# One kernel, two stages: a new order for k's copies, token ranks and early weights, and the last two batches routed together

## The chip, the cores and the metric

The kernel runs on one core of a Trainium2 chip. The metric is device time in microseconds of one execution, 669.85 us as the median of three runs (667.71 to 671.05). The engines are named as the profile names them: PE (TensorE, matrix multiply; PEld is its weight load), DVE (VectorE), ACT (ScalarE), POOL (GpSimd), SP (SyncE, which here issues transfers). Each engine works through its own instructions in order.

## The reference

Two stages. The first is an attention over 8 batches, 8 heads, 576 positions of 64 numbers, done twice and added: once on means of four neighbouring positions (144 coarse positions, all against all, repeated four times), once between positions less than four apart. The second is a mixture of experts on the 4608 tokens of 512 numbers that come out: each token goes to one of 8 experts.

```python
def sm_attn(qq, kk, vv):                       # softmax(qq kk^T / 8) vv
    ...
out_up = np.repeat(sm_attn(q_d, k_d, v_d), 4, axis=2)      # *_d: means of four positions
mask = np.abs(pos[:, None] - pos[None, :]) < 4
out_local = softmax(where(mask, q k^T / 8, -1e9)) @ v
x = (out_up + out_local).transpose(0, 2, 1, 3).reshape(4608, 512)

logits = x @ w_gate + modality_bias[modality_id]
e_idx, gate_w = argmax(logits), max(softmax(logits))
for e in range(8):
    mask = e_idx == e
    h = np.maximum(x[mask] @ w1[e], 0.0)       # 512 -> 1024
    out[mask] = gate_w[mask, None] * (h @ w2[e])           # 1024 -> 512
```

## The kernel before

**The attention** runs in 32 steps of two heads each (four steps, n = 4b to 4b+3, are one batch b). What one step's heads need is spread over several steps, so that the engines work on different steps at once. The order is written by hand: `PHASE` gives each operation a time in units of a step, a call for step n gets the time n + phase, all calls are sorted by it, and each engine's instructions are issued in this order. The names that matter:

- `tpq`, `tpk`, `tpt`: PE transposes q and k into PSUM; `qT`, `kT`: ACT copies them into SBUF (`kT0` copies k in two halves of 64 partitions, L330); `kd`: DVE sums k by four.
- `sc`, `lm`, `le`, `exp`, `z`, `zr`, `nl`, `lt`, `Pw`, `avl`: the local part (scores on PE, maximum and difference on DVE, exponential on ACT, sums and their reciprocal on DVE, normalisation `nl` on POOL L426, a DVE transpose, a copy on ACT L442, the product with v on PE).
- `scd`, `dm`, `de`, `nd`, `pdt`, `PdT`, `avd`, `Od`: the same for the coarse part (`nd` on POOL L430, `pdt` PE transposes, `PdT` ACT copies). `vp`, `vc`: v's means. `X`: DVE adds both parts into the tile X of the batch (and `late`, the columns kept for the next batch).
- Routing of a batch, at phases of 7 and more, so some four steps behind its first head: `lg` (PE, the logits in two halves), `LT` (ACT copies), `lgt` (PE transposes), `L`, `ch1`, `ch2`, `gt` (small DVE instructions), `ex` (ACT), `pr` (PE, the rank of each token inside its expert), `pl` (DVE, its place), `st` (POOL: one indirect transfer a tile of 128 tokens, which scatters token number and gate into the table `tab`), `R` (DVE transposes X back to rows of tokens) and `W` (SP stores these rows into `xs`).

Some tiles of PSUM and SBUF turn in rings (tag T with three buffers, S with three, A with two), and an operation waits until the reader of the buffer's last content is done.

**The experts.** After four batches the tokens of the first half are counted (`first`, `early`), and an expert with many of them gets its first two units of 512 tokens early: `expert` and `entries` fetch its number and its list, `rows` gathers the tokens (POOL), `wload` and `wsplit` load its weights in eight chunks, c = 0 to 3 for the first layer, 4 to 7 for the second, and split each into a high and a low part (high on POOL for the first four, else on ACT L876; low on DVE L882). `split` turns the tokens' rows on PE and splits them. `raws` says which buffer (raw0 to raw2) a pair of chunks takes. Chunks with a turn from `HOLD` to `NHOLD` are issued behind the last batch's routing on ACT and DVE. Before, chunks 0 to 3 are handled in the attention and 4 to 7 after it; batch six is routed in the hand-written order, batch seven after it.

`compute` is a unit's first layer: eight blocks f of twelve matmuls (L1005) into PSUM, each followed by a relu on ACT (L1010) and its low part on DVE (L1011); `second` is the second layer (L1059), with a scaled copy (L1061) and an indirect transfer of the result. Then come three units of 1024 tokens (`Large`), two of 256 and one of 128, and a loop for what is left. Outside the hand-written part a planner with its own model of costs orders the instructions.

Of the kernel before, what the change touches and what calls it, by code (L numbers as in the profile page):

```python
# [7 lines left out]
F32 = mybir.dt.float32  # L8
# [4 lines left out]
ALU = mybir.AluOpType  # L13
# [34 lines left out]
NPW = 3  # L48
NR = 4
TB, SB = 3, 3  # L50
HOLD = 5
NHOLD = 8

QUADS = 3
# [4 lines left out]


PHASE = {
# [10 lines left out]
}  # L72


def whole(pieces):

    while True:
        try:
            next(pieces)
        except StopIteration as x:  # L80
            return x.value
# [116 lines left out]
class Attention:  # L198
# [120 lines left out]

    def kT_(s, n, i):  # L320
        g = n % 2
        p = s.t["tp", "t"][:, 1] if i else s.t["tp", "k", n]
        for a in range(2):
            r = slice(64 * a, 64 * a + 64)
            if i:
                t = s.kB[r].rearrange("m g a t -> m g (a t)")[:, :, KT * a + PAD : KT * a + PAD + 512 + 64]
                s.nc.scalar.copy(t[:, 0, 512:], p[r, :64])
                s.nc.scalar.copy(t[:, 1, :64], p[r, 64:])
            else:
                s.nc.scalar.copy(s.kB[r, g, a, PAD + 64 * g : PAD + 64 * g + 512], p[r])  # L330
# [167 lines left out]
class Router:  # L498
# [32 lines left out]
    def LT(s, b, hf):  # L531
        W = 64 * s.t["G", b]
        if ("LT", b) not in s.t:
            s.t["LT", b] = s.wk.tile([128, 640], F32, name="LT", bufs=1)
        s.nc.scalar.copy(s.t["LT", b][:, hf * W : (hf + 1) * W], s.t.pop(("lg", b, hf)))

    def lgt(s, b, i):
# [77 lines left out]
    def R(s, b, t):  # L615

        if t < s.t["G", b]:
            if t % 2 == 0:
                if b < B - 1:
                    x = s.rp.tile([128, 8, 4, 32], F32, name="R", bufs=NR)  # L620
                elif t == 4:
                    x = s.rp.tile([128, 4, 4, 32], F32, name="o", bufs=3)
                else:
                    x = s.block(f"G{2 + t // 2}", F32)[:, :1024].rearrange("p (i k c) -> p i k c", i=8, k=4)
                s.t["R", b, t // 2] = x
            R = s.t["R", b, t // 2][:, 4 * (t % 2) : 4 * (t % 2) + 4]
            s.nc.vector.transpose(R, s.t["X", b][:, :, 128 * t : 128 * t + 128].rearrange("p k (i j) -> p i k j", j=32))
# [178 lines left out]
class Moe:  # L806
    def __init__(s, tc, ctx, C, psum, xs, tab, w1, w2, out):
        s.tc, s.nc, s.C, s.ps = tc, tc.nc, C, psum
        s.xs, s.tab, s.w1, s.w2, s.out = xs, tab, w1, w2, out
        s.wr = ctx.enter_context(tc.tile_pool(name="mwr", bufs=1))  # L810
        s.wa = ctx.enter_context(tc.tile_pool(name="mwa", bufs=1))
        s.xa = ctx.enter_context(tc.tile_pool(name="mxa", bufs=1))
        s.turn = {}
        s.cw, s.after, s.before = 0, (), []
        s.raws = iter([0, 1, 2, 0] + [0, 2, 1] * 6)
        ring = ["G0", "G1", "G2", "G3", "H0", "H1", "H2", "H3", "V0", "V1", "V2", "V3", "H6", "H7"]
        s.wseq = iter(["H4", "H5", "H6", "H7", "V0", "V1", "V2", "V3"] + ring * 3)

# [168 lines left out]
    def compute(s, T, W, X, H=2, step=None, mid=None, J=None, last=0):  # L987
        nc = s.nc
        xh, xl = X
        hh, hl = s.hidden(H)  # L990
        N = 128 * H
        n = 4 // H
        early = H == 4 and s.turn["h"] == 0
        ps = {}
        for f, ks in [(f + j, k) for f in range(0, 8, 2) for k in ((0, 1), (2, 3)) for j in range(2)] if early else [
                (f, range(4)) for f in range(8)]:
            if step and f % 2 == 0 and 0 in ks:
                step()
            if f % n == 0 and 0 in ks:
                ps[f // n] = s.ps.tile([128, n, N], F32, name="l1", tag="S", bufs=SB)  # L1000
            p, fs = ps[f // n], slice(128 * f, 128 * f + 128)
            for k in ks:
                wh, wl = W[k]
                for i, (a, x) in enumerate(((wh, xh), (wh, xl), (wl, xh))):
                    nc.tensor.matmul(p[:, f % n, :], a[:, fs], x[:, k, :N], start=(k == 0 and i == 0),  # L1005
                                     stop=(k == 3 and i == 2))
            if f % n == n - 1 and 3 in ks:
                g = slice((f + 1 - n) % 4, f % 4 + 1)
                y, z = hh[f // 4][:, g, :N], hl[f // 4][:, g, :N]
                nc.scalar.activation(y, p, AF.Relu)  # L1010
                nc.vector.scalar_tensor_tensor(z, p, 0.0, y.bitcast(F32), op0=ALU.max, op1=ALU.subtract)  # L1011
        s.second(T, W[4:], hh, hl, H, step, mid, J, last)

    def compute_half(s, T, W, X, step, mid, J):
# [183 lines left out]
def build(tc, q, k, v, mid, w_gate, bias, w1, w2, out):  # L1198
    nc = tc.nc
    with ExitStack() as ctx:  # L1200
# [10 lines left out]
        with ExitStack() as actx:  # L1211
# [35 lines left out]
            def call(at, f, *args):  # L1247
                calls.append((at, len(calls), f, args))
# [8 lines left out]
            for nm, p in P.items():  # L1257
                f, i = (nm[:-1], int(nm[-1])) if nm[-1].isdigit() and nm not in ("ch1", "ch2") else (nm, 0)
                if f in batch:
                    for b in range(B - 1):  # L1260
                        late_ = {2: 0.05, 0: 0.9, 3: 0.14}.get(i, 0) if f == "st" and b == B - 2 else 0
                        call(4 * b + p + late_, getattr(ro, parts.get(f, f)), b, i)
                else:
                    for n in range(0, N, 2 if f in ("vp", "vc", "tpt") or nm in ("qT1", "kT1", "kd1") else 1):
                        call(n + p, values if f == "X" else getattr(at, parts.get(f, f)), n, i)
            for b in range(B):
                if b + 1 < B:
                    for j in range(2):
                        call(4 * b - 1 + used + 0.3 + 0.8 * j, at.load_v, b + 1, 4 * j)
            for h in range(3, N // 2):  # L1270
                call(2 * h - 5 + last + 0.25, at.load_qk, h // 2, h % 2)

# [57 lines left out]
            for u in range(KEARLY):  # L1330
                call(t + 1 + 0.1 * u, expert, u)
            for u in range(KEARLY):
                call(t + 1.5 + 0.1 * u, entries, u)
            for i in range(4):
                call(t + 4.75 + 0.3 * i, rows, 0, i)
            free = N - 1 + max(P["scd"], P["sc0"], P["sc1"]) + 0.02

            w = max(t + 5, 4 * (B - 2) - 1 + used + 1.1 + 0.8)
            for c in range(4):
                call(w - 1.5 + 0.5 * c, wload, c)  # L1340
            for c in range(2):
                for j in range(2):
                    call(w + 1.5 + 0.6 * c + 0.25 * j, wsplit, c)
            calls.sort(key=lambda x: x[:2])
            with tc.manual_schedule():
                for x in calls:
# [5 lines left out]
            end = N - 1 + P["nd"] + 0.12  # L1352
            for c, j, at_ in ((2, 0, end), (2, 1, end + 0.05), (3, 0, end + 0.06), (3, 1, end + 0.08)):
                call(at_, wsplit, c)
            for j in range(13):
                call(free + 0.4 + 0.15 * j, split, 0)
            calls.sort(key=lambda x: x[:2])
# [7 lines left out]
            with tc.high_priority():  # L1365
                clear(1)
                for h in range(4):
                    rows(1, h)
            b = B - 1
            with tc.high_priority():  # L1370
                for f, k in ((ro.lg, 2), (ro.LT, 2), (ro.lgt, 2), (ro.L, 2), (ro.ch1, 1), (ro.ex, 1), (ro.ch2, 1), (ro.gt, 1)):
                    for i in range(k):
                        f(b, i)
                cnt = whole(ro.counts("m"))
                ro.pr(b, 0)
                ro.pl(b, 0)
                for i in range(5):
                    ro.st(b, i)
            moe.after = ro.last_act, ro.last_dve
            for i in range(5):  # L1380
                ro.R(b, i)
                if i in (1, 3, 4):
                    ro.store(b, i // 2)
            early = [E[0] + [W], E[1]]

        order = [("e", i, 4) for i in range(KEARLY)] + [("q", i, 8) for i in range(NQ)]
# [51 lines left out]
        Es[0], Ts[0], Rs[0], Xs[0], Ws[0] = early[0]  # L1438
        Es[1], Ts[1], Rs[1] = early[1]
        Ws[1] = Ws[0]  # L1440
        for c in range(4, 8):
            Ws[0].append(moe.chunk(Es[0], c))
        todo, raws = [(i, c) for i in range(small, N) for c in range(8)], []
        toload = list(todo)

# [6 lines left out]
        for i, (_, u, H) in enumerate(order):  # L1452
# [12 lines left out]
            if i < KEARLY:  # L1465
                turn = [0]

                def early_step():
                    if i == 1:
                        Xs[2].put(first[turn[0]] if turn[0] < len(first) else "")  # L1470
                    turn[0] += 1

                def mid(h):
# [117 lines left out]
```

## Time and profile before

| | |
|---|---|
| median of three runs | 669.85 us (667.71 to 671.05) |
| the profiled execution | 665.86 us, its span 664.2 us |
| busy PE | 624.9 us, 94% of the span |
| busy DVE, ACT, POOL | 444.3, 387.3, 338.8 us |
| mean granted PE clock | 0.993 of full speed |

The span is from the first to the last instruction. Busy times are sums of the instructions' durations; a matmul's end is modelled, so a busy PE is not PE at its peak. The attention takes the first 250 us, with the engines all busy; the expert part behind it is PE's alone.

### The profile page before, as it was taken

How to read it: one execution, taken by the hardware profiler on the slowest of the kernel's cores; microseconds unless marked ns; L12 is line 12 of the kernel's file. 1: busy time of each engine (PE TensorE's matmuls, PEld its weight loads, DVE VectorE, ACT ScalarE, POOL GpSimd, SP SyncE). 2: the span in 40 equal slices, each digit the busy share in tenths (PEclk: the TensorE clock that was granted, in tenths of full speed). 3: DMA queues.
4: the chain of work that ended last, by engine and by line, in shares of the span. 5: the costliest groups of instructions: out<-in, count | busy, mean ns of one | idle time of the engine just before them, and what ended most of it. 6: DMA issues, size and time to landing. Idle time of an engine off the chain costs nothing. (4 is left out here: it accounts for less than half of the span.)

```text
span 664.2 us, 16573 instructions
## 1 busy us (share of the span) xinstructions
PE 624.9 (94%) x6131; PEld 497.9 (75%) x6131; DVE 444.3 (67%) x977; ACT 387.3 (58%) x902; POOL 338.8 (51%) x378
## 2 busy tenths in 40 slices
PE   8898989998998879899999999999999999999996
PEld 5676666766666657688888888888888878889794
DVE  6788898989889985644446773758728966236610
ACT  4888989987898863412354742438324473346610
POOL 6634645627376747143049776397775730141211
PEclk9999999998999998999999999999999999999999
DMA  8999898999999936459003435224351245549400
GB/s 188 208 183 196 142 187 159 195 189 159 177 138 203 145 92 174 130 129 226 28 33 104 107 87 158 55 97 106 95 163 65 86 105 154 163 126 292 141 16 33
DMA packets 168862, 90.24 MB, mean 136 GB/s; under 512 B 131812, under 2 KB 153354, under 8 KB 168778
## 3 DMA queue, kind: packets, MB, share of 16 engines
q1 hardware_dynamic: 160810, 69.96, 50.0%
q0 software_dynamic: 7968, 19.18, 9.3%
q8 instruction: 50, 0.82, 0.6%
q14 instruction: 34, 0.28, 0.2%
HBM read 69.86 MB, written 19.51 MB: 135 GB/s over the span
## 5 line engine op out<-in xcount | busy, mean ns | idle before, releaser
L1059 PE MATMUL l<-V,H 128*128 128x512 f32 x792 | 184.3, 391 | 0.0
L1059 PEld LDWEIGHTS l<-V,H 128*128 128x128 f32 x792 | 147.8, 188 | 30.6
L945 POOL DMA_INDIRECT xg<-xs,m x64 | 74.9, 1170 | 19.2 <-issue 19.2
L426 POOL TENSOR_TENSOR le<-le,zr 128x384 f32<-128x384 f32 x32 | 26.6, 833 | 86.3 <-DVE zr L422 73.2
L1069 POOL DMA_INDIRECT out_dram<-o,tq x24 | 26.8, 1116 | 76.6 <-ACT o L1061 48.2
L442 ACT COPY Pw<-lt 32x288 f32<-32x288 f32 x128 | 54.6, 426 | 3.7 <-DVE er L712 1.2
L1005 PE MATMUL l<-X,H 128*128 128x512 f32 (+1 forms) x240 | 54.0, 376 | 2.2 <-DVE H L1011 2.2
L1061 ACT ACTIVATE o<-l,tq 128x512 f32<-128x512 f32 x24 | 16.5, 688 | 60.5 <-PE l L1059 39.5
L642 POOL DMA_INDIRECT tab<-ig,si x36 | 38.2, 1062 | 23.3 <-DVE mbase L784 17.1
L1005 PEld LDWEIGHTS l<-X,H 128*128 128x128 f32 x240 | 42.0, 190 | 10.7 <-DVE H L1011 2.5
L1162 ACT ACTIVATE H<-o 128x512 fp32r<-128x512 f32 x36 | 22.8, 634 | 37.7 <-DVE o L1184 37.7
L481 PE MATMUL avl<-Pw,vw 128*64 128x96 f32 x768 | 39.7, 252 | 4.6 <-ACT Pw L442 4.6
L481 PEld LDWEIGHTS avl<-Pw,vw 128*64 128x64 f32 x768 | 33.2, 138 | 12.6 <-ACT Pw L442 7.4
L882 DVE TENSOR_TENSOR V<-raw,V 128x1024 fp32r<-128x1024 f32 x22 | 30.9, 1423 | 13.1 <-ACT V L876 13.1
L330 ACT COPY kT<-tp 64x512 f32<-64x512 f32 x64 | 37.0, 579 | 2.5 <-PE tp L294 1.4
L1011 DVE SCALAR_TENSOR_TENSOR H<-l,H 128x512 fp32r<-128x512 f32 x24 | 16.4, 688 | 32.3 <-ACT H L1010 32.0
L1069 POOL DMA_INDIRECT out_dram<-o,tg x10 | 12.0, 1198 | 48.2 <-ACT o L1061 35.9
L412 ACT ACTIVATE de<-scd,dm 128x144 f32<-128x144 f32 x96 | 35.3, 376 | 1.9
L372 PE MATMUL sc<-kT,qT 128*24 128x64 f32 x1536 | 34.5, 223 | 0.9 <-ACT kT L330 0.9
L344 DVE TENSOR_REDUCE kd<-tp 128x128 f32<-128x512 f32 x32 | 21.4, 670 | 17.4 <-ACT kT L330 15.6
L372 PEld LDWEIGHTS sc<-kT,qT 128*24 128x24 f32 x1536 | 24.5, 103 | 10.6 <-issue 4.2
L1010 ACT ACTIVATE H<-l 128x512 fp32r<-128x512 f32 x24 | 14.2, 596 | 31.1 <-PE l L1005 31.1
(281 smaller groups left out, 1463.4 us busy)
## 6 DMA issues: line engine op xcount, KB each, us to landing
raw<-in_moe_w_dram SPq DMA_DIRECT2D x112, 128.0 KB
raw<-in_moe_w_dram SPq DMA_DIRECT2D x28, 512.0 KB
vw<-in_v_dram SPq DMA_DIRECT2D x60, 180.0 KB
qt<-in_q_dram SPq DMA_DIRECT2D x26, 288.0 KB
kt<-in_k_dram SPq DMA_DIRECT2D x26, 288.0 KB
xs<-R SPq DMA_DIRECT2D x56, 128.0 KB
qt<-in_q_dram SPq DMA_DIRECT2D x6, 256.0 KB
kt<-in_k_dram SPq DMA_DIRECT2D x6, 256.0 KB
```

Source lines behind the costliest of these rows:

```text
L330: s.nc.scalar.copy(s.kB[r, g, a, PAD + 64 * g : PAD + 64 * g + 512], p[r])
L372: s.nc.tensor.matmul(p[32 * j : 32 * j + SUB, 2 * i : 2 * i + 2, :], qT[:, q0 : q0 + SUB], kB[:, :, q0 : q0 + WIN], start=False, stop=(i = ...
L412: s.nc.scalar.activation(x, s.t["scd", n][:, c].rearrange("p (k x) -> p k x", k=NB), AF.Exp, bias=m[:, c : c + 1], accum_out=s.t["z", n][: ...
L426: s.nc.gpsimd.tensor_tensor(e, e, z[:, : 2 * NB].unsqueeze(2).broadcast_to([128, 2 * NB, WIN]), op=ALU.mult)
L442: s.nc.scalar.copy(s.Pw[n % NPW][r, :, j, :SUB], s.t["lt", n][r, :, :SUB])
L481: s.nc.tensor.matmul(p[64 * a : 64 * a + 64, c], vw[:, NB * (4 * (hp // 2) + hp % 2 + 2 * a) + k, :], Pw[:, 2 * k + a], start=True, stop=T ...
L642: i = nc.gpsimd.indirect_dma_start(out=s.tab[:, :], out_offset=bass.IndirectOffsetOnAxis(ap=C.si[:, t : t + 1], axis=0), in_=C.ig[:, t, :] ...
L882: (nc.gpsimd if turn == 4 else nc.vector).tensor_tensor(lo, raw, hi.bitcast(F32), op=ALU.subtract)
L945: s.nc.gpsimd.indirect_dma_start(out=R[l].rearrange("p h (i x) -> p (h i) x", i=4)[:, i, :], out_offset=None, in_=s.xs.rearrange("n (a x) ...
L1005: nc.tensor.matmul(p[:, f % n, :], a[:, fs], x[:, k, :N], start=(k == 0 and i == 0), stop=(k == 3 and i == 2))
L1059: nc.tensor.matmul(p, l, x[:, f % 2, :], start=(f == 0 and i == 0), stop=(f == 7 and i == 2))
L1069: nc.gpsimd.indirect_dma_start(out=s.out[:, :], out_offset=bass.IndirectOffsetOnAxis(ap=T[:, h, 0:1], axis=0), in_=o, in_offset=None, boun ...
```

## The change

- `kT0` now copies only the first half of k, at 0.1900, and a new `kT2` the second half at 0.2050. The first copy of `LT` stands at 7.1923, so between them in the steps with routing.
- `pr` and `pl` go from 7.84 and 7.93 to 8.10 and 8.13; all five `st` stand behind `nd` (x.5956) and `qe`.
- The two loads of v for batch 7 come 1.39 and 0.78 of a step earlier. The entries of the early units, the gathers of the first unit's rows and the loads of weight chunks 0 to 3 come later, the loads one step apart (phases 28.3, 29.3, 30.3, 31.3), and chunks 0 and 1 are split in the last step.
- Chunks 4 to 7 are loaded from the hand-written order, into raw0 and raw1 again (`raws`), and 4 and 5 are split at its end. `HOLD` goes from 5 to 7, so that only 6 and 7 are held.
- Batch six's routing (lg to st) leaves the hand-written order and is done with batch seven's, operation by operation.
- The rows (`R`, `store`) of both batches are done inside the first unit's `compute`, one pair of tiles at each of five of its steps, behind the last `low` issued.

```diff
-HOLD = 5
+HOLD = 7
...
-"tpt": 0.1888, "kT0": 0.2050, "qT1": 0.5097,
+"tpt": 0.1888, "kT0": 0.1900, "kT2": 0.2050, "qT1": 0.5097,
...
-    "R4": 7.7000, "gt": 7.8318, "pr": 7.8428, "pl": 7.9316, "st4": 9.0000, "W2": 8.5000, "R1": 8.2990, "W0": 9.1000,
-    "st2": 8.5946, "st0": 8.6238, "R2": 9.2990, "st3": 9.5946, "st1": 10.2000, "R3": 10.2990, "W1": 11.1000,
+    "R4": 7.7000, "gt": 7.8318, "pr": 8.1000, "pl": 8.1300, "st4": 9.6238, "W2": 8.5000, "R1": 8.2990, "W0": 9.1000,
+    "st2": 8.6300, "st0": 8.6238, "R2": 9.2990, "st3": 9.6300, "st1": 10.6300, "R3": 10.2990, "W1": 11.1000,
...
-        s.raws = iter([0, 1, 2, 0] + [0, 2, 1] * 6)
+        s.raws = iter([0, 1, 0, 1] + [0, 2, 1] * 6)
...
-                nc.vector.scalar_tensor_tensor(z, p, 0.0, y.bitcast(F32), op0=ALU.max, op1=ALU.subtract)
+                s.low = nc.vector.scalar_tensor_tensor(z, p, 0.0, y.bitcast(F32), op0=ALU.max, op1=ALU.subtract)
...
-                    for b in range(B - 1):
-                        late_ = {2: 0.05, 0: 0.9, 3: 0.14}.get(i, 0) if f == "st" and b == B - 2 else 0
-                        call(4 * b + p + late_, getattr(ro, parts.get(f, f)), b, i)
+                    for b in range(B - 2):
+                        call(4 * b + p, getattr(ro, parts.get(f, f)), b, i)
...
-                        call(4 * b - 1 + used + 0.3 + 0.8 * j, at.load_v, b + 1, 4 * j)
+                        late_ = (1.39, 0.78)[j] if b == B - 2 else 0
+                        call(4 * b - 1 + used + 0.3 + 0.8 * j - late_, at.load_v, b + 1, 4 * j)
...
-                call(t + 1.5 + 0.1 * u, entries, u)
-            for i in range(4):
-                call(t + 4.75 + 0.3 * i, rows, 0, i)
+                call(4 * (B - 2) + 1.3 + 0.01 * u, entries, u)
+            for i, x in enumerate((0.64, 1.64, 2.64, 2.66)):
+                call(4 * (B - 1) + x, rows, 0, i)
...
-            w = max(t + 5, 4 * (B - 2) - 1 + used + 1.1 + 0.8)
             for c in range(4):
-                call(w - 1.5 + 0.5 * c, wload, c)
+                call(4 * (B - 1) + 0.3 + c, wload, c)
             for c in range(2):
                 for j in range(2):
-                    call(w + 1.5 + 0.6 * c + 0.25 * j, wsplit, c)
+                    call(N - 1 + (0.15, 0.66)[c] + 0.25 * j, wsplit, c)
...
+            for c in range(4, 8):
+                call(N - 1 + (1.7 if c < 6 else 3.9) + 0.01 * c, wload, c)
+            x0, od = N - 1 + P["X0"], N - 1 + P["Od"]
+            for c, at_ in ((4, od + 0.01), (5, od + 0.02)):
+                call(at_, wsplit, c)
+                call(x0 + 0.1 * c, wsplit, c)
...
+                last = range(B - 2, B)
+                for fs in ((ro.lg, ro.LT), (ro.lgt, ro.L)):
+                    for b, i in [(b, i) for b in last for i in range(2)]:
+                        for f in fs:
+                            f(b, i)
+                for f in (ro.ch1, ro.ex):
+                    for b in last:
+                        f(b, 0)
+                for b in last:
+                    ro.ch2(b, 0)
+                    ro.gt(b, 0)
+                    if b == B - 1:
+                        cnt = whole(ro.counts("m"))
+                    ro.pr(b, 0)
+                    ro.pl(b, 0)
+                    for i in range(5):
+                        ro.st(b, i)
             moe.after = ro.last_act, ro.last_dve
-            for i in range(5):
-                ro.R(b, i)
-                if i in (1, 3, 4):
-                    ro.store(b, i // 2)
...
-        for c in range(4, 8):
-            Ws[0].append(moe.chunk(Es[0], c))
+        for c in (6, 7):
+            Ws[0].append(whole(moe.wsplit(raw[c], c)))
...
+                    elif 0 < turn[0] < 6:
+                        b, t = ((B - 2, 0), (B - 2, 1), (B - 1, 0), (B - 1, 1), (B - 1, 2))[turn[0] - 1]
+                        with tc.issue_after(moe.low.ins):
+                            for j in range(2):
+                                ro.R(b, 2 * t + j)
+                        ro.store(b, t)
```

Two tiles change with it: batch six's LT takes a buffer of the later ring `o`, and the rows of the two batches lie in the blocks G2 and G3, two pairs in each.

## Rows read from the trace of the kernel before

**Rows 1.** Busy time by stage: us, then each engine's busy us (instructions), clock, DMA, GB/s.

```profile
50.00:226.00 176.00, 158.19 (x3103) 118.19 (x3099) 158.11 (x500) 155.88 (x491) 101.85 (x132) 0.99 0.97 172
226.00:251.00 25.00, 19.29 (x318) 13.82 (x313) 21.41 (x61) 18.29 (x55) 12.67 (x16) 0.96 0.50 103
251.00:282.00 31.00, 28.76 (x155) 21.94 (x152) 18.55 (x65) 10.21 (x17) 11.87 (x11) 0.97 0.57 163
282.00:620.00 338.00, 337.95 (x1557) 280.40 (x1557) 199.79 (x240) 156.05 (x218) 175.58 (x151) 1.00 0.43 122
```

**Rows 2.** TensorE's waits, 58 to 226 us: us in total, times, longest.

```profile
PE lgt L541 <- ACT LT L535: 4.3, 5, 0.9
...
PE pdt L451 <- POOL de L430: 2.8, 5, 1.1
...
PE pr L593 <- DVE late L492: 1.5, 3, 0.7
PE pr L593 <- DVE X L492: 1.3, 3, 0.4
```

**Rows 3.** Timeline, ScalarE, a routing step: start us, us, instruction, [idle before <- releaser].

```profile
81.59 0.42 ACT L535 COPY LT<-lg 128x320 f32<-128x320 f32 x1 [0.77 <-PE lg L528]
81.91 1.19 ACT L330 COPY kT<-tp 64x512 f32<-64x512 f32 x2
```

**Rows 4.** Timeline, TensorE, the same step and the next.

```profile
83.60 0.55 PE L541 MATMUL lgt<-ident,LT 128*128 128x128 f32 x3 [0.86 <-ACT LT L535]
...
88.19 0.19 PE L593 MATMUL pr<-oh,tri 128*128 128x40 bf16 x1 [0.44 <-DVE late L492]
...
94.84 0.61 PE L451 MATMUL pdt<-ident,de 64*96 64x64 f32 x12 [0.61 <-POOL de L430]
```

**Rows 5.** Timeline, VectorE, the same steps.

```profile
83.13 0.69 DVE L344 TENSOR_REDUCE kd<-tp 128x128 f32<-128x512 f32 x1 [1.45 <-ACT kT L330]
...
94.68 0.67 DVE L284 COPY vd<-vp 96x512 f32<-96x512 f32 x1
```

**Rows 6.** Timeline, GpSimd, between nl and nd.

```profile
92.85 1.00 POOL L642 DMA_INDIRECT tab<-ig,si  x1 [0.15 <-ACT kT L328]
```

**Rows 7.** TensorE's waits, 226 to 282 us.

```profile
PE l L1005 <- DVE H L1011: 2.2, 1, 2.2
PE pdt L451 <- POOL de L430: 1.5, 2, 1.0
PE pr L593 <- DVE X L492: 1.1, 1, 1.1
...
PE lgt L541 <- ACT LT L535: 0.9, 1, 0.9
```

**Rows 8.** Timeline, GpSimd, steps 28 to 31.

```profile
209.13 0.82 POOL L426 TENSOR_TENSOR le<-le,zr 128x384 f32<-128x384 f32 x1 [5.32 <-DVE zr L422]
...
220.79 2.00 POOL L642 DMA_INDIRECT tab<-ig,si  x1 [0.16 <-issue]
...
229.86 0.83 POOL L426 TENSOR_TENSOR le<-le,zr 128x384 f32<-128x384 f32 x1 [3.24 <-ACT kT L330]
```

**Rows 9.** Timeline, VectorE, beside that scatter.

```profile
220.67 1.23 DVE L882 TENSOR_TENSOR H<-raw,H 128x1024 fp32r<-128x1024 f32 x1 [0.83 <-POOL H L876]
```

**Rows 10.** Timelines of SP and ScalarE, second layer's weights.

```profile
258.70 6.75 SPq L636 DMA_DIRECT2D xs<-G  x8
...
271.52 1.05 ACT L876 CAST V<-raw 128x1024 fp32r<-128x1024 f32 x1 [5.53 <-DMA raw<-in_moe_w_dram]
```

**Rows 11.** VectorE by line, 251 to 282 us; timelines of VectorE, GpSimd and TensorE.

```profile
L627 DVE STREAM_TRANSPOSE G<-X 128x512 f32<-128x512 f32 x4 | 2.5, 680 | 1.7 <-DMA xs<-R 1.7
...
265.26 0.20 DVE L571 TENSOR_REDUCE mw<-w 128x5 f32<-128x40 f32 x1
...
296.21 1.01 POOL L937 DMA_INDIRECT xg<-xs,tq  x1 [0.30 <-issue]
...
311.37 0.38 PE L965 MATMUL xt<-ident,xg 128*128 128x128 f32 x2
```

More of the change, by code (lines that the diff above doesn't have):

```diff
@@ L321, in kT_ @@
         g = n % 2
-        p = s.t["tp", "t"][:, 1] if i else s.t["tp", "k", n]
-        for a in range(2):
+        p = s.t["tp", "t"][:, 1] if i == 1 else s.t["tp", "k", n]
+        for a in (0, 1) if i == 1 else (i // 2,):
             r = slice(64 * a, 64 * a + 64)
-            if i:
+            if i == 1:
                 t = s.kB[r].rearrange("m g a t -> m g (a t)")[:, :, KT * a + PAD : KT * a + PAD + 512 + 64]
@@ L533, in LT @@
         if ("LT", b) not in s.t:
-            s.t["LT", b] = s.wk.tile([128, 640], F32, name="LT", bufs=1)
+            s.t["LT", b] = (s.rp.tile([128, DM], F32, name="o", bufs=3) if b == B - 2 else
+                            s.wk.tile([128, 640], F32, name="LT", bufs=1))
         s.nc.scalar.copy(s.t["LT", b][:, hf * W : (hf + 1) * W], s.t.pop(("lg", b, hf)))
@@ L618, in R @@
             if t % 2 == 0:
-                if b < B - 1:
+                if b < B - 2:
                     x = s.rp.tile([128, 8, 4, 32], F32, name="R", bufs=NR)
@@ L623, in R @@
                 else:
-                    x = s.block(f"G{2 + t // 2}", F32)[:, :1024].rearrange("p (i k c) -> p i k c", i=8, k=4)
+                    if t == 0:
+                        s.two = s.block(f"G{b - B + 4}", F32)
+                    x = s.two[:, 512 * t : 512 * t + 1024].rearrange("p (i k c) -> p i k c", i=8, k=4)
                 s.t["R", b, t // 2] = x
@@ L1368, in build @@
                     rows(1, h)
-            b = B - 1
             with tc.high_priority():
[L1371 to L1376, printed above, removed]
-                for i in range(5):
-                    ro.st(b, i)
+                last = range(B - 2, B)
[15 more added lines that the diff above has]
+                        ro.st(b, i)
             moe.after = ro.last_act, ro.last_dve
-            for i in range(5):
-                ro.R(b, i)
-                if i in (1, 3, 4):
-                    ro.store(b, i // 2)
             early = [E[0] + [W], E[1]]
```

2 rows, old and new, of the table PHASE are left out of this document.

## The prediction

> **What bounds the kernel now.** I read the busy time by stage first [rows 1]. From 282 to 620 us TensorE is busy 337.95 of 338 us: in the expert part it sets the time alone, and whatever makes it get there earlier comes off the end one for one, as long as nothing there is waiting for something that does not move along. Before 282 us it is not alone. In the attention (50 to 226 us) TensorE, VectorE and ScalarE are busy 158.2, 158.1 and 155.9 of 176 us, all three about 90%, and a gap on one of them is often the lateness of another. At the end of the attention (226 to 251 us) TensorE has 19.3 of 25 us, in the first layer (251 to 282 us) 28.8 of 31. So I looked for TensorE's gaps before 282 us, and for each asked which engine was truly late.
>
> The waits by total name them [rows 2]: the router's transposes wait for ScalarE's copy LT five times for 4.3 us between 58 and 226 us (0.86 each, and a sixth time ahead of that window), the rank matmuls (pr) wait for VectorE's X and late six times, 2.8 us, the transposes of the coarse weights (pdt) wait for GpSimd's normalisation 2.8 us. Most stand in every fourth step, the one in which a batch is routed, or right behind it.
>
> **K's copies.** In the routing step at 79 us ScalarE ends q's copy at 80.82, sits idle 0.77 us until the first lg is summed, copies LT, then copies k's two halves (1.19 us, to 83.10), then the second LT [rows 3]. Two engines wait for this: TensorE's second lgt, at 83.60, 0.86 us [rows 4], and VectorE's sum kd, which stands idle 1.45 us until k's copies end [rows 5]. The change puts k's first half (phase 0.19) ahead of LT (0.1923). It needs only k's transposes, which TensorE does ahead of lg, so half of the 1.19 us, 0.58 with the overlap of the two taken off, fits into the idle 0.77. The second half, the second LT, lgt and kd then all come 0.58 us earlier. That counts, since behind kd VectorE runs without a gap to speak of until 95 us, and the copies on ScalarE and the matmuls behind are hung on it. Six batches have it (the seventh leaves this place): 6 x 0.58 = 3.5 us. Bounds: 0, if the gap moves to the next wait; 6 x 0.86 = 5.2. I take 3.5, because the three engines that could hold it are all shifted.
>
> **Ranks and scatters.** pr goes from before the next step's transposes to behind them. Its wait is for the two A buffers of PSUM that X reads (0.44 us at 88.19 [rows 4]); 0.25 of a step later X is done. The scatters of a batch now all stand behind nd in GpSimd's order; today one of 1.00 us stands between nl and nd (92.85 [rows 6]), and pdt waits 0.61 us for it. Together these waits are 2.8 + 2.8 us [rows 2]. I do not count them so: VectorE is the late one there. The next step's q transposes need the buffer that vc frees at 95.35, at the end of VectorE's unbroken chain [rows 5], so TensorE would only wait there instead. I take 0.5; bounds 0 and 5.6.
>
> **Steps 28 to 31.** Batch six's lg, lgt and rank matmuls leave step 31 and are issued later, where TensorE is full: the same instructions at the same price, no gain and no loss. With them go the waits of 0.9 and 1.1 us [rows 7]. But the gathers of the first expert's rows (four, each about 1.0 us and 0.3 of issue as in [rows 11]; today they stand ahead of 5.32 us in which GpSimd is idle [rows 8]) come to steps 28 to 30, between the scatters of batch five. From nl at 209.13 to the nl at 229.86 are 20.7 us, 3.24 of them idle [rows 8]. New: less the idle 3.2, less one weight cast that now comes later (1.0, an estimate from ScalarE's cast of that size [rows 10]), less 1.0 for the slow scatter, plus 4 x 1.3 for the gathers: 20.7 us. So GpSimd has no idle time left there, and pdt, which follows nl and nd, can come no earlier than this chain lets it: the 0.9 is likely turned into a wait for nd. I take 1.0, the wait of pr; bounds 0 and 2.8 (both waits, and a pdt wait of the 0.8 us that they average).
>
> There is a row that speaks against this place. The scatter at 220.79 took 2.00 us where the one at 92.85 took 1.00, and it stood beside VectorE's subtraction raw minus H of 1.23 us at 220.67 [rows 6, 8, 9]. The two such subtractions of the early weights now fall beside nl and nd of step 31. By the Trainium skill ("SBUF — State Buffer", Who interferes with whom) a VectorE instruction with two SBUF inputs blocks a GpSimd one that reads SBUF for its whole length, so that nl and nd could be held too; the page thinks that it would not hold an indirect transfer's issue, where this trace shows just that. No nl or nd of this trace stands beside such a subtraction. By the rule the sum would be up to 1.0 us smaller.
>
> **The tail of the attention.** TensorE is idle 5.7 us between 226 and 251 us [rows 1]; without the 2.0 of lgt and pr 3.7 remain. It follows z, zr, nl, nd, pdt, PdT, avd of the last two steps, with only the transposes of the expert's rows to fill. pdt's two waits for nd make 1.5 us, the longer one 1.0 [rows 7], and between the last nl and nd stands a scatter of batch six as in [rows 6], 1.0 us, which goes. VectorE loses batch six's routing (eighteen instructions of about 0.2 us, 3.4 [rows 11]) and four transposes, and gets two subtractions of 1.2 [rows 9] from the steps before. I take 1.0; bounds 3.7 and -2.0 (lgt's and pr's waits come back here). The granted clock of the two stretches is 0.96 and 0.97, so TensorE was at its 1.2 GHz level for a small part of them; I leave that as it is.
>
> **The first layer's stall.** TensorE stands 2.2 us there for VectorE's H [rows 7]. The chain: SP issues one load of the second layer's weights, then eight stores of batch seven's rows that wait for their transposes and hold it from 258.70 to 265.45, and only then the other loads; ScalarE, in order, waits 5.53 us for the transfer until 271.52, then does three casts of 1.05 us between its relus [rows 10]; the layer's sums fill PSUM and TensorE stops. In the change four of these loads are issued from the attention, two at phase 32.7, two at 34.9, the first two are split there, and rows go to SP later, one pair at a time. The late transfer is gone. I take 2.2; bounds 0 and 2.2.
>
> **What the first layer gets.** VectorE has there batch six's routing besides batch seven's (3.4 us each), and nine row transposes (0.68 us [rows 11]) instead of five, behind the `low` of the columns before. Its load in 251 to 282 us is 18.55 of 31 us [rows 1]; plus 3.4 and 2.7, less two subtractions now done earlier (2.4): 22.3. It fits, and a low has the time of one buffer to spare; I take -0.5, bounds 0 and -9.5 (the whole of nine transposes, 6.1, and of one routing, 3.4, on TensorE's path). The scatters become nine, each 1.0 us and 0.3 of issue, on a GpSimd that is busy 11.87 of 31 us there; and the rows that hang on them are gathered up to 297 us and first turned at 311 [rows 11]. So nothing there.
>
> **Sum:** 3.5 + 0.5 + 1.0 + 1.0 + 2.2 - 0.5 = 7.7 us. The profiled execution took 665.86 us (span 664.2 and 1.7 around it): 658.2. It lies 4.0 us under the median of the three runs shown (669.85), and what is read here does not depend on that, so I carry the difference over: 669.85 - 7.7 = 662.2.
>
> **Rivals.**
> A: the attention keeps nothing. The 0.58 us come back as a longer wait for nd, as today's 2.8 us of pdt [rows 2] show that it can be. Against it: kd, the start of VectorE's chain, moves too. Then 1.0 + 1.0 + 2.2 - 0.5 = 3.7: 666.2.
> B: the stall stays. The last two loads need a buffer whose second half GpSimd subtracts at the very end of the attention, and the casts stand ahead of the relus in ScalarE's order as now. Against it: the DMA engines are half idle there (0.50 [rows 1]) and the first two casts are done before the layer. 662.2 + 2.2 = 664.4.
> C, slower: the first layer turns VectorE-bound. Its queue is in order, and a pair of transposes (1.3 us) and a routing of eighteen instructions are put in front of lows on which PSUM's three buffers hang. Price: 6.1 + 3.4 = 9.5 on the path and the stall kept, against 6.0 from the other parts: 669.85 + 3.5 = 673.4. For it: summed over the layer VectorE comes to within a few us of TensorE's time. Against it: there are 12 us of idle VectorE now, and some of the transposes fall into the second layer. It decides once TensorE's idle time in that layer passes 2.2 + 6.0 = 8.2 us.
>
> **How the numbers follow.** Forecast 0.57, A 0.17, B 0.14, C 0.12. The forecast's own range is 657 to 666. To hold 8 in 10 the range takes in A and B and the better bounds of the middle parts (some 6 us more): 656 to 668.5. About 0.5% (3.3 us) is what a measurement of this kernel can tell from no change. Faster than 666.5: 0.55 of the forecast, half of A, most of B: 0.76. Within: 0.14. Slower than 673.2: most of C, whose waits would also lower the clock, 0.10.
>
> **What would show it.** In the routing steps ScalarE's idle time ahead of LT falls to about 0.1, kd's wait from 1.45 to 0.9 and lgt's from 0.86 to 0.3; else A. pdt in step 29 waits for nd, with GpSimd full from 206 us on. No wait of ScalarE for raw in the first layer and no idle TensorE above 0.5 us there; else B, or C if the releaser is VectorE's H behind transposes. Wrong altogether if the expert part, 282 to 620 us today, gets longer.

## The result, and the profile after

The changed kernel takes 674.83 us (median of 20 runs, 670.31 to 678.10), the kernel before 670.49 in the 20 runs beside it: ratio 1.006, interval 1.0039 to 1.0081. The forecast of 662.2 is missed on the other side, and its range with it. The profiled execution took 673.67 us (span 672.0). Ratios and intervals here and below leave out the runs on record as slow, medians do not.

Busy time by stage, as in [rows 1]:

```profile
50.00:226.00 176.00, 156.26 (x3041) 115.08 (x3038) 154.51 (x493) 156.31 (x483) 95.40 (x128) 1.00 0.89 167
226.00:251.00 25.00, 19.85 (x345) 14.48 (x346) 19.12 (x45) 17.95 (x56) 15.07 (x18) 1.00 0.73 164
251.00:282.00 31.00, 30.67 (x199) 22.91 (x199) 21.23 (x68) 11.68 (x24) 9.82 (x8) 1.00 0.38 108
282.00:620.00 338.00, 333.54 (x1524) 276.53 (x1523) 196.72 (x257) 152.46 (x215) 182.53 (x157) 0.99 0.42 119
```

The first layer is full (30.67 of 31, where it was 28.76), but the expert part, which had 337.95 of 338, now stands idle 4.46 us: what the prediction had named as "wrong altogether". It is one wait of TensorE, in the first layer of the second unit. Timelines of the kernel before (SP, ScalarE, GpSimd's last scatter), then of the changed kernel (with TensorE):

```profile
288.15 0.38 SPq L894 DMA_DIRECT2D tq<-tab  x1
288.77 8.09 SPq L851 DMA_DIRECT2D raw<-in_moe_w_dram  x16
...
303.73 1.05 ACT L1122 CAST G<-raw 128x1024 fp32r<-128x1024 f32 x1 [5.58 <-DMA raw<-in_moe_w_dram]
...
284.42 0.96 POOL L642 DMA_INDIRECT tab<-ig,si  x1 [0.30 <-issue]
```

```profile
295.76 0.40 SPq L897 DMA_DIRECT2D tq<-tab  x1
296.41 9.04 SPq L854 DMA_DIRECT2D raw<-in_moe_w_dram  x16
...
313.98 1.04 ACT L1125 CAST G<-raw 128x1024 fp32r<-128x1024 f32 x1 [8.14 <-DMA raw<-in_moe_w_dram]
314.94 1.56 ACT L1013 ACTIVATE H<-l 128x512 fp32r<-128x512 f32 x3
...
281.39 1.06 POOL L645 DMA_INDIRECT tab<-ig,si  x1 [20.13 <-DVE mni L667]
...
291.70 1.13 POOL L645 DMA_INDIRECT tab<-ig,si  x1 [0.30 <-issue]
...
317.06 7.14 PE L1008 MATMUL l<-X,H 128*128 128x512 f32 x19 [4.43 <-DVE H L1014]
```

Read it backwards. TensorE stands 4.43 us for VectorE's H; that needs the relus, which ScalarE does in order, behind a cast that waits 8.14 us for weights. These 16 loads stand behind the list read (tq) on SP, as before; but the list waits for the scatters, and these are nine, until 292.83, where they were five, until 285.38. So the loads start 7.6 us later. In the kernel before the cast waited for weights too, but was over ahead of the unit's first relu. A spell at half clock follows the stall: the granted clock of 300 to 320 us is 0.89, of 320 to 340 us 0.94, where both were 1.00.

In the routing steps the profile shows what was forecast. The step of [rows 3 to 5]:

```profile
82.16 0.58 ACT L330 COPY kT<-tp 64x512 f32<-64x512 f32 x1
82.92 0.42 ACT L536 COPY LT<-lg 128x320 f32<-128x320 f32 x1 [0.18 <-PE lg L528]
...
83.98 0.69 DVE L344 TENSOR_REDUCE kd<-tp 128x128 f32<-128x512 f32 x1 [0.85 <-ACT kT L330]
...
84.45 0.55 PE L542 MATMUL lgt<-ident,LT 128*128 128x128 f32 x3 [0.38 <-ACT LT L536]
```

LT's idle time fell from 0.77 to 0.18 us, kd's wait from 1.45 to 0.85, lgt's from 0.86 to 0.38. Yet this execution gained nothing by it. Where the time is, by stage (differences of start times in the timelines: the q transposes of steps 0, 24, 28 and 31, the last avl, the first matmul of the second layer, the end of the span). The runs e1 to e14 are told in the next section. Each row is one execution: that of the kernel before, 665.86 us, lies 4.6 us under the median above, that of e1, 665.59 us, 6.6 us under e1's own.

| execution, us | 0 to 24 | 24 to 28 | 28 to 31 | 31 to last avl | to second layer | to the end |
|---|---|---|---|---|---|---|
| before | 170.9 | 28.5 | 20.5 | 27.0 | 27.2 | 383.8 |
| changed | 172.4 | 28.8 | 25.3 | 22.2 | 27.3 | 390.2 |
| changed, again (e1) | 167.0 | 27.9 | 20.4 | 26.7 | 27.3 | 388.3 |
| e3 | 170.3 | 33.4 | 23.2 | 26.3 | 26.6 | 383.8 |
| e4 | 168.2 | 34.2 | 22.4 | 27.2 | 26.6 | 384.9 |
| e8 | 168.6 | 27.8 | 21.4 | 23.9 | 27.3 | 385.2 |
| e10 | 166.1 | 34.5 | 21.1 | 27.0 | 25.9 | 384.0 |
| e11 | 169.1 | 28.9 | 21.8 | 23.2 | 27.3 | 388.5 |
| e12 | 166.2 | 28.3 | 21.2 | 23.8 | 26.0 | 386.0 |
| e14 | 170.4 | 28.5 | 20.2 | 30.6 | 24.6 | 383.6 |

In the changed kernel's first execution TensorE's waits of 58 to 226 us [rows 2] have moved: lgt's are 1.9 us instead of 4.3 and pr's gone, but the transposes wait longer for PdT (2.5 us before):

```profile
PE tp L298 <- ACT PdT L459: 6.3, 10, 1.5
...
PE lgt L542 <- ACT LT L536: 1.9, 5, 0.4
```

And step 30 took 11.4 us instead of 7.0. TensorE's matmuls come there in small groups, with gaps for which the profile shows no wait, while GpSimd issues two gathers back to back and SP eight weight loads (225.92 to 231.46). Timelines of GpSimd, TensorE and VectorE, changed kernel:

```profile
228.40 1.04 POOL L940 DMA_INDIRECT xg<-xs,tg  x1 [0.30 <-issue]
...
229.76 1.01 POOL L940 DMA_INDIRECT xg<-xs,tg  x1 [0.31 <-issue]
...
230.61 0.28 PE L372 MATMUL sc<-kT,qT 128*24 128x64 f32 x3 [0.50 <-issue]
...
231.35 0.39 PE L372 MATMUL sc<-kT,qT 128*24 128x64 f32 x9 [0.47 <-issue]
231.42 0.39 DVE L492 TENSOR_TENSOR X<-avl,Od 128x224 f32<-128x224 f32 x1 [2.29 <-remote]
```

### The profile page after: what moved, and what is told of

Its sections match the earlier page's. It is cut to its first block, busy times and chain, and to the rows that moved or that the text cites. A ratio compares the mean times of both kernels' runs of the same rounds, so it can differ in the third digit from the quotient of the medians.

```text
span 672.0 us, 16567 instructions
## 1 busy us (share of the span) xinstructions
PE 629.0 (94%) x6131; PEld 499.4 (74%) x6131; DVE 443.9 (66%) x977; ACT 389.5 (58%) x902; POOL 339.1 (50%) x378
## 5 line engine op out<-in xcount | busy, mean ns | idle before, releaser
L948 POOL DMA_INDIRECT xg<-xs,m x64 | 76.5, 1195 | 19.2 <-issue 18.6
L426 POOL TENSOR_TENSOR le<-le,zr 128x384 f32<-128x384 f32 x32 | 26.6, 830 | 92.9 <-DVE zr L422 62.6
L1072 POOL DMA_INDIRECT out_dram<-o,tq x24 | 27.3, 1137 | 74.4 <-ACT o L1064 52.6
L1008 PE MATMUL l<-X,H 128*128 128x512 f32 (+1 forms) x240 | 56.2, 386 | 4.4 <-DVE H L1014 4.4
L1008 PEld LDWEIGHTS l<-X,H 128*128 128x128 f32 x240 | 43.5, 197 | 13.1 <-DVE H L1014 4.7
L645 POOL DMA_INDIRECT tab<-ig,si x36 | 36.1, 1003 | 26.9 <-DVE mni L667 20.1
L885 DVE TENSOR_TENSOR V<-raw,V 128x1024 fp32r<-128x1024 f32 x22 | 33.0, 1524 | 9.5 <-ACT V L879 8.8
L1126 DVE TENSOR_TENSOR G<-X,G 128x1024 fp32r<-128x1024 f32 x15 | 23.3, 1551 | 21.5 <-ACT G L1125 21.3
```

The costliest lines, as they stand in the source:

```text
L426: s.nc.gpsimd.tensor_tensor(e, e, z[:, : 2 * NB].unsqueeze(2).broadcast_to([128, 2 * NB, WIN]), op=ALU.mult)
L645: i = nc.gpsimd.indirect_dma_start(out=s.tab[:, :], out_offset=bass.IndirectOffsetOnAxis(ap=C.si[:, t : t + 1], axis=0), in_=C.ig[:, t, :] ...
L885: (nc.gpsimd if turn == 4 else nc.vector).tensor_tensor(lo, raw, hi.bitcast(F32), op=ALU.subtract)
L948: s.nc.gpsimd.indirect_dma_start(out=R[l].rearrange("p h (i x) -> p (h i) x", i=4)[:, i, :], out_offset=None, in_=s.xs.rearrange("n (a x) ...
L1072: nc.gpsimd.indirect_dma_start(out=s.out[:, :], out_offset=bass.IndirectOffsetOnAxis(ap=T[:, h, 0:1], axis=0), in_=o, in_offset=None, boun ...
```

## The experiments

Each ratio is to the kernel before in runs on the same chip; edits are to the changed kernel unless said.

**e1: the changed kernel again; e2: the second unit's loads first.**

```diff
-                            gather(2)
+                            Es[2] = moe.expert(lists["q"][1], 0)
+                            Xs[2] = Large(moe, Es[2], None, None, 0)
                             Xs[2].put("l0 l1")                         # weight loads
+                            Ts[2] = moe.entries(lists["q"][0], 0, 8)   # list, then gathers
...
```

> The changed kernel as it is, a second execution to look into. Theory (the late loads cost it): the ratio to the kernel before is 1.004 to 1.008 again, TensorE stands 4 to 4.5 us once near 317 us in the second unit's first layer, for VectorE's H behind casts that wait for the raw weights, and then runs some 7 us at 1.2 GHz. Rival (the attention costs it): that stall is absent or under 1 us, and step 30 of the attention again takes 11 us, not 7. If step 30 takes about 7 us here and the stall is there, the 4.4 us of step 30 were of that one execution.

> The changed kernel with the expert's number and the first two weight loads of the second unit put ahead of that unit's list of rows and its gathers in SyncE's order. Theory: the loads no longer wait for the nine scatters; the 4.4 us of TensorE's stall and some 3.4 us of half clock behind it go: 4.4 to 7.8 us under the changed kernel, ratio to the kernel before 0.995 to 1.000. Rival (the attention costs it, or VectorE in that layer): within 1 us of the changed kernel, ratio 1.005 to 1.007.

e1: 672.19 us, ratio 1.0107 (1.0063 to 1.0151); its six runs go from 665.59 to 679.59 us, and the trace is of the lowest. The stall is there (3.27 us at 309.69), while step 30 took 6.6 us: the first second-layer matmul starts at 275.5, 4.8 us earlier than before where 7.7 were forecast, and the stages behind it lose 4.5. e2: 666.85 us, 0.9987 (0.9962 to 1.0012). The late loads cost 5.3 us by these two medians, 8 by the two ratios (0.0120 of 667.5).

In e2's trace (674.49 us) the wait for the weights is gone, but another has come: the list is now read behind the loads, and TensorE waits 1.83 us for the second unit's rows (3.18 in e11). In step 30, which took 14.9 us there, TensorE waits for V. TensorE, e2:

```profile
223.29 1.93 PE L279 MATMUL vp<-vw,pool 128*32 128x256 f32 x12 [6.03 <-DMA vw<-in_v_dram]
...
319.69 0.44 PE L968 MATMUL xt<-ident,xg 128*128 128x128 f32 x2 [1.83 <-DMA xg<-xs,tq]
```

**e3, e4: the kernel before with one part alone.** e3 has only the two phases of k's copies, e4 only the places of ranks and scatters.

```diff
-"kT0": 0.2050,                                     # e3
+"kT0": 0.1900, "kT2": 0.2050,
...
-"pr": 7.8428, "pl": 7.9316, "st4": 9.0000, ...     # e4
+"pr": 8.1000, "pl": 8.1300, "st4": 9.6238, ...
```

> The kernel before with k's first half copied ahead of LT and nothing else. The prediction's step: 3.5 us faster, ratio 0.995. Rival A (the gap moves to another wait of the same steps): LT's idle time and kd's wait shrink, the steps behind the routing steps get longer by as much, and the ratio is 0.999 to 1.002.

> The kernel before with the rank matmuls and the five scatters of a batch at their new places and nothing else. The prediction's step: 0.5 us faster, ratio 0.999. The bound above it: 5.6 us, ratio 0.992, if pdt's and pr's waits both go for good. Rival A: pr's wait goes, pdt or the next q transposes wait as long for VectorE, ratio 0.999 to 1.002.

e3: 0.9975 (0.9955 to 0.9995), 1.7 us: half of the forecast. Its trace (671.61 us, the highest of 13 runs) gains 0.6 us over steps 0 to 24, and a gather in step 27 waits 7.49 us. With k's copies and the old ranks the wait that went comes back at other places. TensorE's waits of 58 to 226 us in e14 (told below), which has k's copies and the old ranks too:

```profile
PE pdt L451 <- POOL de L430: 3.8, 6, 1.1
...
PE pr L593 <- DVE late L492: 2.0, 3, 1.1
PE lgt L541 <- ACT LT L535: 1.9, 5, 0.4
PE pr L593 <- DVE X L492: 1.9, 3, 0.6
```

Against [rows 2] lgt's wait has lost 2.4 us, while pdt's has gained 1.0 and pr's 1.1. With the new ranks neither pr's wait nor pdt's for GpSimd is in this list (e1); pdt waits 4.0 us for VectorE instead. All waits of lgt, pdt and pr named here sum to 9.9 us in the kernel before, 9.6 in e14 and 5.9 in e1.

e4: 1.0063 (1.0025 to 1.0100), slower by 4. Its trace gains 2.7 us over steps 0 to 24 (168.2) and loses 5.8 in steps 24 to 28: a gather in step 27 waits 6.08 us, and the normalisations and pdt (2.62 us) behind it.

**e5 to e7: fewer loads; e8: the loads first, ranks and scatters at their old places.** The first three add this to the kernel before, the changed kernel and e4:

```diff
 def load_v(s, b, part, W=4):
+    if 2 <= b <= 6:
+        return
```

> The kernel before with V's loads of batches two to six left out (the buffers keep batches 0 and 1, so these batches are computed from other values), which takes some 40 of the 50 V loads off SyncE's queue between 20 and 200 us. Theory L (SyncE's queue, which issues for 160 to 169 of these 180 us, sets how early loads come): the runs lie closer together, none more than 1% above the lowest, and the median is 1 to 4 us under the kernel before. Rival E (the engines set the attention alone, loads don't matter): the same median within 1 us and the same spread.

> The changed kernel with the same V loads left out. Theory L: the attention's 4.8 us of gain now shows in every run and only the second unit's stall and half clock (4.5 to 6.5 us) stand against it: within 2 us of the light kernel before, no run over 1% above the lowest. Rival E: it stays 4 us or more above the light kernel before, as the changed kernel stands above the kernel before.

> The kernel before with the ranks and scatters at their new places and the same V loads left out. Theory L: with loads in time the new places gain what the steps up to 26 showed, 2 to 3 us under the light kernel before. Rival E (the new places cost engine time): 4 us or more above the light kernel before, as with all loads.

> The changed kernel with the second unit's weight loads ahead of its list, and ranks and scatters back at their places of before. Theory L: the stores of routed rows wait less for VectorE's transposes, so the loads behind them come earlier: 2 to 4 us under the same kernel with the new ranks, ratio to the kernel before 0.993 to 0.997, and fewer of the runs over 670 us. Rival: ranks only cost by themselves and not here, ratio 0.998 to 1.002.

e5: 1.0009 (0.9976 to 1.0042): the kernel before has nothing from fewer loads. e6: 1.0102 (1.0043 to 1.0161), e7: 1.0127 (1.0075 to 1.0179). Theory L failed in all three, and what rival E said came: the median of e5 is within 1 us of the kernel before, those of e6 and e7 lie 7.1 and 8.5 us above e5. In e6 the trace shows why: the stall is 5.20 us, and step 30 takes 10.3 with gaps of 0.47 us as above. For e7 it shows only where: in step 27 VectorE and ScalarE wait 2.54 and 3.07 us for something that the profile doesn't name. The gather of that step no longer waits (e4: 6.08 us), and still the step takes 13.3 us. e8: 666.79 us, 0.9973 (0.9936 to 1.0010), hardly different from e2. Its second unit has no wait for weights, but its rows come a little late, as in e2 (TensorE waits 1.1 us at 306.38). SP and ScalarE, e8:

```profile
286.45 9.14 SPq L854 DMA_DIRECT2D raw<-in_moe_w_dram  x16
296.45 0.39 SPq L897 DMA_DIRECT2D tq<-tab  x1
...
300.55 1.05 ACT L1125 CAST G<-raw 128x1024 fp32r<-128x1024 f32 x1 [3.56 <-DMA tq<-tab]
```

**e9: batch six back in the attention; e10: e2 with the first gathers in steps 27 and 28; e11: e10 with the old ranks.**

```diff
-last = range(B - 2, B)                                          # e9, and its calls in the attention back
+last = range(B - 1, B)
-for i, x in enumerate((0.64, 1.64, 2.64, 2.66)): call(4 * (B - 1) + x, rows, 0, i)
+for i in range(4): call(26.97 + 0.3 * i, rows, 0, i)            # e10, with entries at 23.72
```

> The changed kernel, but batch six's routing, scatters and rows back in the hand-written order of the attention; only batch seven's stand beside the first layer. Theory S (the four more scatters and the later slots hold the second unit's list, and the list holds its weight loads on SyncE): TensorE's stall near 310 us in the second unit falls from 3.3 to 5.2 us to under 1.5, and the kernel is 4 to 7 us under the changed one, ratio to the kernel before 0.995 to 1.002. Rival W (the early second-layer weights, with their turn of buffers, make it): the stall stays at 3 us or more and the ratio at 1.006 to 1.011.

> The changed kernel with the second unit's weight loads ahead of its list, and the four gathers of the first expert's rows back in steps 27 and 28, ahead of the early weights' loads and not beside them. Theory G (gathers issued back to back beside eight weight loads hold up TensorE's instructions in step 30): step 30 takes 7 us in the trace, no gap of TensorE without a wait above 0.4 us there, and the time is 2 to 4 us under the kernel with only the loads first: ratio to the kernel before 0.993 to 0.997. Rival Q (the list of the first expert is read late on SyncE): the gather at step 27 waits up to 7 us, GpSimd's normalisation and pdt behind it, ratio 1.000 to 1.006.

> The same with ranks and scatters at their old places too: what is left of the change is k's copies, the early weights, the joint routing, and the loads first. Theory G: 2 to 4 us under the kernel with old ranks and the gathers late (0.9973), ratio 0.991 to 0.995, the fastest so far. Rival Q: the gather waits in step 27, ratio 0.997 to 1.003.

e9: 0.9980 (0.9954 to 1.0007): without the joint routing there is no wait for the weights either (none in the traces of e9, e13 and e14), as theory S says. e10: 0.9975 (0.9949 to 1.0001), e11: 0.9969 (0.9944 to 0.9994); neither came to what G promised, and e11 loses 3.18 us to the wait for rows. In e10 step 30 is 6.6 us, as G has it, but Q happened in step 27, which took 14.7. Timelines of SP, GpSimd and TensorE, e10, and below it the first two in the kernel before:

```profile
195.29 1.61 SPq L897 DMA_DIRECT2D tg<-tab  x2
...
200.35 1.04 POOL L940 DMA_INDIRECT xg<-xs,tg  x1 [8.26 <-DMA xs<-R]
...
205.77 0.87 PE L451 MATMUL pdt<-ident,de 64*96 64x64 f32 x12 [6.29 <-POOL de L430]
```

```profile
185.42 1.87 SPq L894 DMA_DIRECT2D tg<-tab  x2
...
196.00 1.07 POOL L937 DMA_INDIRECT xg<-xs,tg  x1 [0.69 <-DMA qt<-in_q_dram]
```

The steps run 4 us ahead of the kernel before, and SP reaches the list 10 us later than there, with as many transfers ahead of it. SP works in order and is nearly full: its transfer instructions between 20 and 200 us sum to 160 us in the kernel before and to 161 to 169 in the others that leave no load out. That it is the faster steps which make the list late is not shown: e3 and e14 have as many transfers ahead of the list and the same pace (170.3 and 170.4 us for steps 0 to 24), yet read it 15 us apart. SP in e3, below it in e14:

```profile
197.97 1.62 SPq L894 DMA_DIRECT2D tg<-tab  x2
...
182.93 1.62 SPq L896 DMA_DIRECT2D tg<-tab  x2
```

From 120 to 170 us 154 GB/s were moved in e3 and 170 in e14; why is open.

**e12, e13: the same fewer loads, in kernels without the stall (e10 and e9); e14: k's copies and the early weights alone.** e14 is e9 with ranks and gathers at the places of before; batch seven's rows stay inside the first unit.

> The kernel with the second unit's weight loads ahead of its list and the gathers back in steps 27 and 28, and V's loads of batches two to six left out (those batches are computed from other values). Theory L2 (the 4 to 4.8 us that steps 0 to 24 gain are lost again in steps 26 to 31 to transfers that SyncE issues late): no wait for a transfer or for a gather in steps 24 to 31, the attention keeps its gain, 3 to 5 us under the kernel with all loads (0.9975): ratio 0.990 to 0.994. Rival M (the loss has nothing to do with the loads): ratio 0.996 to 1.003.

> The kernel with batch six back in the attention's order, and the same V loads left out. Theory L2: no wait for a transfer in steps 24 to 31, 3 to 5 us under the same kernel with all loads (0.998): ratio 0.990 to 0.995. Rival M: ratio 0.996 to 1.003, with other waits of the same size in the place of those for transfers.

> The kernel before with k's copies and the early weights (and the earlier V loads) alone: ranks, gathers and batch six at their places of before. The prediction's terms for these parts, 3.5 for k's copies and 2.2 for the first layer's stall: ratio 0.9915. By what the runs have shown (k's copies 0.6 to 2.3 us, the stall of the first layer 2.2 to 2.6, no stall in the second unit): 3 to 5 us, ratio 0.993 to 0.996. Rival: the gain of k's copies is lost to the gather in step 27, ratio 0.996 to 0.999.

e12: 659.72 us, 0.9901 (0.9877 to 0.9924), below e10's interval, and the trace has no wait for a transfer left in steps 24 to 31:

```profile
173.00 1.56 SPq L899 DMA_DIRECT2D tg<-tab  x2
...
193.27 1.04 POOL L942 DMA_INDIRECT xg<-xs,tg  x1 [0.30 <-issue]
```

The list is read 22 us earlier than in e10 and the gather doesn't wait. Of the five kernels with fewer loads this is the one that is clearly faster for it. e13: 0.9952 (0.9936 to 0.9968), 1.9 us better than e9, less than L2 said, and the intervals overlap. e14: 664.08 us, 0.9943 (0.9918 to 0.9968), as expected: with all its work it beats the kernel before by 3.8 us. Its first layer and expert part have no hole (below), but the tail ahead of them took 30.6 us instead of 27.0, with a gap of TensorE of 2.29 us ahead of 227.88 for which the profile names no wait. So its trace is only 0.4 us shorter than that of the kernel before (spans 663.8 and 664.2), and does not show where the 3.8 us of the medians come from.

```profile
251.00:282.00 31.00, 30.13 (x188) 23.38 (x187) 22.62 (x64) 13.38 (x24) 16.04 (x13) 1.00 0.45 122
...
282.00:620.00 338.00, 337.99 (x1559) 280.52 (x1558) 200.96 (x244) 156.35 (x217) 175.72 (x151) 1.00 0.43 123
```

## Why the prediction was wrong

**The step that failed** is the last sentence on the first layer. It followed the nine scatters to the rows that hang on them, found these first turned at 311 us, and concluded "So nothing there". The scatters hold the list, and the list is read on SP, in front of the second unit's first weights. The prediction had itself argued by a queue's order ("Its queue is in order", of VectorE), and had the pattern in [rows 10]: a transfer held up by stores on SP, and casts ahead of relus on ScalarE. It did not ask what else stands behind the list on SP. Forecast 0; 6.4 us behind the first layer in the first execution and 4.5 in e1, 5.3 to 8 by e1 and e2. Two edits at different links of this chain, e2 and e9, each remove the wait for the weights: this is shown. The whole miss is 12.0 us (7.7 faster forecast, 4.3 slower measured), so gains that did not come or did not stay are the rest.

**K's copies and ranks, 4.0 together.** The waits for LT and kd shrank as said, but both terms were mis-sized over steps 0 to 24. K's copies were to bring 3.5 and gained 0.5 and 0.6 alone (e14, e3; 1.9 and 2.3 with the joint routing and the old ranks, e11 and e8), for pdt's and pr's waits grew. The ranks were to bring 0.5, since TensorE would only wait for VectorE instead, and gained 2.7 alone (e4): it does wait for VectorE, but less. Together they gained 3.9 (e1) and 4.8 and 4.7 (e10, e12), near the 4.0 forecast: that the sum fits is luck. In the first execution and e6 they gained nothing, and fewer loads did not change that.

What failed as well is that the gain would stay. [Rows 1] says 0.97 for the DMA engines in this stage, higher than TensorE's 0.90, and here the prediction read only the three compute engines. That late transfers take the gain back is shown for e10 against e12 alone. Against it as a rule stand e7, whose step 27 is as long without a late list, and e5, where the same loads cost the slower kernel before nothing. That k's copies alone bring 1.7 us and ranks alone lose 4 also speaks against adding the terms up.

**Steps 28 to 31 and the tail, 2.0.** In e1 0.4, in the first execution 0: its 4.8 us less from step 31 on are the 4.8 more of steps 28 to 31. The forecast wait for nd in step 29 came in neither. What step 30 lost, in the first execution and in e6, was not forecast. In the tail the prediction priced VectorE's subtractions by their length, 1.2 us each, and not by their wait for the weights. In e1 one of them waits, in order, ahead of the last sums' reciprocal, so that nl, nd and pdt come late. GpSimd, VectorE and TensorE, e1:

```profile
232.61 1.04 POOL L879 CAST H<-raw 128x1024 fp32r<-128x1024 f32 x1 [2.88 <-DMA raw<-in_moe_w_dram]
...
233.68 1.38 DVE L885 TENSOR_TENSOR H<-raw,H 128x1024 fp32r<-128x1024 f32 x1 [2.15 <-DMA xs<-R]
...
237.32 0.54 PE L451 MATMUL pdt<-ident,de 64*96 64x64 f32 x12 [3.00 <-POOL de L430]
```

The early weights' subtractions did fall beside GpSimd's work there: at 235.99 one took 1.55 us, and GpSimd's qd beside it 1.29, where it takes 0.42 at 226.48; nl and nd, at 234.13 and 234.93, missed it and took their usual 0.82 and 0.90. In e1 both stood beside one (225.92 and 226.72) and took 0.83 and 0.90, while the subtraction took 2.71; in e2 an nd beside one (237.05) took 1.88. So the rule of the Trainium skill that the prediction weighed ("SBUF — State Buffer", Who interferes with whom) bears out in kind: one of the two was held, by 0.9 to 1.5 us.

**The first layer, 2.2 less 0.5.** The stall went, as said, and VectorE's 21.2 us fitted: rival C's VectorE-bound layer didn't come. With batch six in the attention the stretch to the second layer is 2.6 us shorter (e14), though the tail ahead of it is 3.6 longer. In the changed kernel it is as long as before, for batch six's matmuls (1.07 us of lg, 0.88 of lgt, 0.3 of ranks) stand in the hole; the prediction counted them as neither gain nor loss, but the attention they left did not get shorter by as much.

**The rivals.** Slower was right by its sign, but C's mechanism was not it. A's outcome came in the first execution. A's cause, a longer wait for nd, shows where the ranks are old (pdt 3.8 us for 2.8, e14); with the new ranks this wait is gone, and the gain was lost to late transfers (e10) or to what stays open. In B's sentence "the casts stand ahead of the relus" stood the very mechanism, one unit too early.

**Left open:** why the changed kernel's first execution and e6 wait longer for PdT from step 8 on, while e1 and e12 don't; what ranks alone lose in e7; why SP reads the list so late in e3 and e10; and whether the gathers cause the gaps of TensorE in step 30. These gaps stand beside two gathers issued back to back in three traces (the first execution and e6 in step 30, e8 in step 31), but e1 has such a pair without them, and e14 a gap of 2.29 us in step 31 without a gather. K's copies and the ranks together, without the rest, were not run.

## What to carry to other kernels

Where a change delays what one transfer waits for, list every transfer that stands behind it on the same queue and follow each to its first reader; here the rows had time to spare and the weights behind them none. When three engines are 90% busy, read the DMA column and the issuing queue too before adding up gains: a stage that gets faster may need its loads earlier (e10 against e12). Price parts in the company they will have: k's copies alone gained 0.6 us in steps 0 to 24, since other waits took the place of the one that went, and on top of the ranks 1.2 to 2.1 (e1 and e10 against e4).

## What the runs showed of the hardware

TensorE can run dry with no wait in the trace: in step 30 of the changed kernel's first execution its matmuls came one to nine at a time, 0.46 to 0.50 us apart. The 16 KB packets of the DMA queue that the profile calls instruction (q8), which start 3.5 to 10.5 us apart between 60 and 212 us, show none between 212.3 and 226.4 us. That late instructions are the cause is not shown: e10 has as long a pause (199.9 to 214.3 us) where TensorE is known to wait for GpSimd, and e6 has the gaps with packets at most 9.7 us apart.

A VectorE subtraction of two SBUF tiles and GpSimd's work beside it stretch one another: 2.71 us for 1.23 (e1), 1.88 for 0.90 (e2), 1.29 for 0.42 (first execution).
